# Other batch sizes, weights converted in wide pieces by a leaky ramp, the last chain on four quadrants, and a new order

## The chip, the cores and the metric

The kernel runs on one core of one Trainium2 chip. The metric is device time in microseconds of one execution, and the figure of a kernel is the median of its runs. The core has a matrix engine (PE, in the profile also TensorE), three engines for element work (DVE or VectorE, ACT or ScalarE, POOL or GpSimd), a queue that issues transfers (SP), and 16 DMA engines. SBUF is the memory that all engines work in; PSUM, eight banks of 512 columns, receives what PE computes.

## The reference

Two attention steps over 4 batches of 12480 tokens with 128 channels, and then a two-layer network on all 49920 tokens:

```python
def mab(q, kv):                      # softmax attention
    s = scale * (q @ kv.transpose(0, 2, 1))
    a = softmax(s)
    return a @ kv
h = mab(I, x)                        # I: 32 inducing rows; h: 32 x 128 per batch
x2 = mab(x, h)                       # 12480 x 128 per batch
y = x2 @ w_in                        # 128 -> 2048
g = 0 if y <= -1; y if y >= 1; (y + 1)**2 / 4 between
out = g @ w_out                      # 2048 -> 128
```

x is float32; w_in and w_out arrive as float64, which no engine computes in.

## The kernel before, in words

Below, "batch" is one of the 4 batches b of the reference, and "chunk" one of the 25 token batches of 512 or 480 into which each b is cut (SIZES); GROUPS joins up to four chunks whose attention is computed side by side in the four quadrants of 32 partitions.

**Weights (load_f32, load_in, load_out).** Each 256-column piece of a float64 weight is fetched as pairs of 32-bit words and turned into float32 by a row of steps: ACT scales the high word (L908), DVE or POOL clamps (L914), DVE shifts (L919), takes the sign bit over from the raw word (L923), masks (L929) and multiplies with the low word (L934), and DVE or POOL joins the two parts (L945 for w_in, L942 for w_out). Then w_out is kept as an fp32 copy w_f (L975) or as an upper and a lower fp32r half, w_hi (L984) and w_lo (L982).

**Summary of a batch (summarize).** Per group: x is loaded (L1008; for b = 0 it is transposed by PE, L1018, and copied by ACT, L1023; for the others it is loaded a second time in 32-column pieces, L1036, and transposed by DVE, L1039), scored against the inducing rows (L1061), its maximum taken (L1066), exponentiated with the group's own maximum (L1078), transposed (L1103, L1113), multiplied with x (L1122) and kept in hs (L1129). After all seven groups a chain of small steps c1 to c12 (L1163 to L1208) finds the maximum over groups, the factor of each group, the sum, and adds the groups up in PE with one matmul for each (L1204). The result is hT (32 summary rows). It is multiplied with w_in (L1230), so that the first layer of the network acts on 32 rows instead of on 128 channels; hw holds the product as fp32r halves, spread by DMA (L1251).

**Attention of a group (attend; attend_first for chunk 0).** Scores, softmax over 32 columns on DVE, ACT and POOL (L1279 to L1322); the weights aT go into chunk rows by DMA (L1346).

**Chunk (chunk).** For each of eight k: two hidden matmuls (L1465), a rectifier on ACT (rise, L1473), a square on ACT (L1459), max and min against the hidden value on DVE (bound, L1478). For k in SPLIT (six of eight; in the very last chunk END, five of eight) the result is split: the upper half hi is written by DVE (L1504), ACT (L1502) or POOL (L1498), the lower half lo by POOL alone (L1509), and PE projects with three fp32r matmuls for each 128 rows (L1540); the other k are projected in fp32 with w_f. A transpose (L1552) and four stores (L1556) end a chunk. Until the first projection PE is kept busy by 128-column matmuls of the identity that nobody reads (L1568).

**What sets the order.** All operations are put down in program order by add(), which names engine, slots and needs. ORDER gives each a rank on its own engine (even numbers; an odd one allows a pair of neighbouring PSUM banks to be handled by one instruction), and ON chooses the engine where there is a choice. Plan.order then emits one queue per engine in that order; every engine works through its queue strictly in order. SLOTS says how many buffers each pool has; FIRST says which pools the 25 first x tiles use. In the first chunk, the lower half on POOL also waits for all eight pieces of w_out (the list ahead).

## Time and profile before

| | us |
|---|---|
| median of 3 runs | 1698.43 (1698.05 to 1699.51) |
| span of the profiled execution | 1695.9 |
| PE busy | 1680.8 (99%) |
| ACT busy | 1643.5 (97%) |
| DVE busy | 1629.2 (96%) |
| POOL busy | 1615.0 (95%) |
| DMA, mean over the span | 62 GB/s, 105.65 MB |

Busy time is the union of instruction durations of an engine; neighbours can overlap, and a matmul's end is modelled. A timeline row gives start and length in us from the start of the span, the line, what is written and read, and in brackets the idle time before it with what ended it. A group row gives the count, then busy time and mean length in ns, then idle time before and its releasers.

### The profile page before, as it was taken

How to read it: one execution, taken by the hardware profiler on the slowest of the kernel's cores; microseconds unless marked ns; L12 is line 12 of the kernel's file. 1: busy time of each engine (PE TensorE's matmuls, PEld its weight loads, DVE VectorE, ACT ScalarE, POOL GpSimd, SP SyncE). 2: the span in 40 equal slices, each digit the busy share in tenths (PEclk: the TensorE clock that was granted, in tenths of full speed). 3: DMA queues.
4: the chain of work that ended last, by engine and by line, in shares of the span. 5: the costliest groups of instructions: out<-in, count | busy, mean ns of one | idle time of the engine just before them, and what ended most of it. 6: DMA issues, size and time to landing. Idle time of an engine off the chain costs nothing.

```text
span 1695.9 us, 24904 instructions
## 1 busy us (share of the span) xinstructions
PE 1680.8 (99%) x7770; PEld 1193.0 (70%) x7770; DVE 1629.2 (96%) x2057; ACT 1643.5 (97%) x2232; POOL 1615.0 (95%) x859
## 2 busy tenths in 40 slices
PE   8999999999999999999999999999999999999998
PEld 6766767677766766677776676677777666667776
DVE  6999999999999999999999999999999999999997
...
GB/s 233 127 53 69 96 66 58 67 60 70 79 67 57 67 64 73 52 68 63 69 87 53 77 52 47 92 54 55 39 33 63 35 24 38 35 28 35 37 28 25
DMA packets 427094, 105.65 MB, mean 62 GB/s; under 512 B 369842, under 2 KB 412434, under 8 KB 426962
## 3 DMA queue, kind: packets, MB, share of 16 engines
...
q8 instruction: 61, 1.00, 0.3%
q14 instruction: 71, 0.58, 0.1%
q10 hardware_dynamic: 1232, 0.40, 0.1%
...
## 4 chain that ended last, share of the span: by engine, by line
PE 79%; DVE 7%; ACT 7%; issue 3%; POOL 2%; SPq 1%; DMA 1%; DVEq 0%; ACTq 0%; POOLq 0%
PE banks L1540 55%; PE banks L1465 17%; DVE w L1478 4%; ACT w L1473 3%; ACT w L1459 3%; DVE hi L1504 2%; PE banks L1122 2%; POOL lo L1509 1%; PE banks L1568 1%; PE banks L1061 1%; PE banks L1279 1%; DVE oT L1552 1%; PE banks L1103 1%; SPq L1036 1%; PE banks L1018 1%
## 5 line engine op out<-in xcount | busy, mean ns | idle before, releaser
L1509 POOL TENSOR_TENSOR lo<-w,hi 128x1024 fp32r<-128x1024 f32 (+1 forms) x599 | 1392.4, 2353 | 17.7 <-PE banks L1540 4.2
L1478 DVE SCALAR_TENSOR_TENSOR w<-banks,w 128x512 f32<-128x512 f32 (+3 forms) x1105 | 953.2, 899 | 19.1 <-ACT w L1459 13.6
L1473 ACT ACTIVATE w<-banks 128x512 f32<-128x512 f32 (+3 forms) x1160 | 814.8, 755 | 12.2 <-PE banks L1465 8.3
L1459 ACT ACTIVATE w<-w 128x1024 f32<-128x1024 f32 (+1 forms) x800 | 820.2, 1054 | 6.4
L1465 PE MATMUL banks<-aT,hw 128*128 128x512 f32 (+1 forms) x1600 | 592.2, 430 | 0.6 <-DVE w L1478 0.4
L1540 PE MATMUL banks<-hi,w_lo 128*128 128x512 f32 (+1 forms) x1198 | 497.4, 415 | 4.0 <-DVE oT L1552 2.9
L1504 DVE TENSOR_REDUCE hi<-w 128x1024 fp32r<-128x1024 f32 (+1 forms) x406 | 475.5, 1179 | 9.0 <-PE banks L1540 0.9
L1540 PE MATMUL banks<-hi,w_hi 128*128 128x512 f32 (+1 forms) x1198 | 462.9, 386 | 0.0
L1540 PE MATMUL banks<-lo,w_hi 128*128 128x512 f32 (+1 forms) x1198 | 460.3, 431 | 1.0 <-DVE oT L1552 0.8
L1465 PEld LDWEIGHTS banks<-aT,hw 128*128 128x128 f32 x1600 | 295.8, 188 | 154.8 <-DVE w L1478 48.5
L1540 PE MATMUL banks<-w,w_f 128*128 128x512 f32 (+1 forms) x804 | 397.5, 581 | 0.0
L1540 PEld LDWEIGHTS banks<-lo,w_hi 128*128 128x128 f32 x1198 | 223.4, 188 | 103.5 <-issue 49.8
L1540 PEld LDWEIGHTS banks<-hi,w_lo 128*128 128x128 f32 x1198 | 225.0, 188 | 89.4 <-issue 27.1
L1540 PEld LDWEIGHTS banks<-hi,w_hi 128*128 128x128 f32 x1198 | 225.1, 188 | 54.6 <-issue 16.0
L1540 PEld LDWEIGHTS banks<-w,w_f 128*128 128x128 f32 x804 | 150.8, 188 | 45.0 <-issue 18.8
L1498 POOL TENSOR_SCALAR hi<-w 128x1024 fp32r<-128x1024 f32 (+1 forms) x141 | 145.4, 1033 | 4.5 <-DVE w L1478 1.4
L1552 DVE STREAM_TRANSPOSE oT<-banks 128x512 f32<-128x512 f32 (+1 forms) x100 | 69.8, 698 | 8.6 <-PE banks L1540 7.5
L1502 ACT CAST hi<-w 128x1024 fp32r<-128x1024 f32 (+1 forms) x52 | 53.6, 1034 | 0.5 <-DVE w L1478 0.5
L1039 DVE STREAM_TRANSPOSE xT<-xr 128x512 f32<-128x512 f32 (+1 forms) x75 | 51.0, 684 | 1.4 <-issue 0.9
L1322 POOL TENSOR_TENSOR a<-a,ahi 128x512 fp32r<-128x512 f32 (+3 forms) x28 | 35.5, 1269 | 1.0 <-ACT ahi L1319 1.0
L1061 PE MATMUL banks<-xT,indT 128*32 128x512 f32 (+1 forms) x200 | 30.5, 592 | 0.0
L1311 POOL TENSOR_TENSOR s<-s,sm 128x512 f32<-128x512 f32 (+3 forms) x28 | 29.0, 1034 | 1.1 <-DVE sm L1308 1.0
(127 smaller groups left out, 545.7 us busy)
## 6 DMA issues: line engine op xcount, KB each, us to landing
out<-oT SPq DMA_DIRECT2D x240, 64.0 KB, 2.2
...
xr<-in_x SPq DMA_DIRECT2D x120, 60.0 KB, 2.4
```

Of the source, the lines that this page charges most:

```text
L1039: nc.vector.transpose(make(xT[b, c])[:, : CW[c]], xr.tile[:, : NB[c]].rearrange("c n i -> c (n i)"))
L1061: nc.tensor.matmul(p[q * M : (q + 1) * M, :cw], indT, xT[b, c].tile[:, :cw], start=True, stop=True)
L1459: nc.scalar.activation(w.tile[:, :, :cw], w.tile[:, :, :cw], AF.Square, scale=0.5)
L1465: nc.tensor.matmul(make(h)[:, :cw], hw[b][ft // 4].tile[:, ft % 4 * P : (ft % 4 + 1) * P], aT[b, c].tile[:, :cw], start=True, stop=True,)
L1473: each(of, i, hs_, lambda h, to: nc.scalar.activation(to, h, AF.Relu, bias=1.0), cw, w)
L1478: lambda h, t: nc.vector.scalar_tensor_tensor(t, h, 1.0, t, op0=ALU.max, op1=ALU.min), cw, w,
L1498: nc.gpsimd.tensor_scalar(make(hi)[:, :, :cw], w.tile[:, :, :cw], 1.0, 0.0, op0=ALU.mult, op1=ALU.add)
L1502: nc.scalar.copy(make(hi)[:, :, :cw], w.tile[:, :, :cw])
L1504: nc.vector.tensor_reduce(make(hi)[:, :, :cw], w.tile[:, :, :cw].unsqueeze(3), axis=AX.X, op=ALU.max)
L1509: nc.gpsimd.tensor_sub(make(lo)[:, :, :cw], w.tile[:, :, :cw], hi.tile[:, :, :cw].bitcast(F32))
L1540: nc.tensor.matmul(acc.tile[:, :cw], wt[k][:, i, :], g.tile[:, i, :cw], start=first, stop=(acc.parts == 0),)
L1552: nc.vector.transpose(make(oT)[:, :nb].rearrange("c n i -> c (n i)"), acc.tile[:, :cw])
```

## The change

SIZES becomes 20 chunks of 512 and 5 of 448 tokens, and the seventh group holds one chunk. For b = 0 every x tile has four token blocks; 448-token chunks order their columns the other way round (n i instead of i n). The first 16 x tiles lie two by two in the hi and lo slots, the other nine in xn, so that the eight w slots take the raw weights. Weights are converted in eight pieces of 512 columns. The scaling step is a leaky ramp (Prelu) with a slope of 2^32 for negative values, so that the shift by three keeps the sign and the step that took it over from the raw word is gone; w_f, w_hi and w_lo are written for two k at once, on ACT or POOL. The copies of x for b = 0 may be on DVE. In the summary, the maximum over the first six groups is taken before the last group is scored; the last group is scored in all four quadrants, so that each has its maximum; the first six groups are added up on DVE (merge, six steps), and two matmuls are left where there were seven. Chunks 0 and 1 use END (five of eight k split), the list ahead is gone, and the square has its factor moved into the rectifier. ORDER and ON are new. In the new ON the uppers of the chunks are 391 on DVE, 66 on ACT and 140 on POOL; the squares stay on ACT; of the 25 copies of x, 13 are on DVE.

Read from the new ORDER, SP issues x0 to x19 of b = 0 (11 and 12 swapped), w_in 0, x20 to x24, w_in 1, 3, 2, w_out 0, 3, 1, 2; POOL makes ident first; DVE's queue from the clamp of w_in 0 to the copy of hT has 39 steps, and ACT's rebias steps stand in five groups between exponentials.

The diff, cut to its core; of ORDER and ON nothing is shown:

```diff
-FIRST = ["w", "hi", "lo"] * 2 + ["xn"] * 9 + ["w", "hi", "w", "lo", "w", "w", "hi", "w", "lo", "w"]
-SIZES = [512] * 15 + [480] * 10
-GROUPS = [[0, 1, 2, 3], [4, 5, 6, 7], [8, 9, 10, 11], [12, 13, 14], [15, 16, 17, 18], [19, 20, 21, 22], [23, 24]]
+FIRST = ["hi"] * 4 + ["lo"] * 4
+SIZES = [512] * 20 + [448] * 5
+GROUPS = [[0, 1, 2, 3], [4, 5, 6, 7], [8, 9, 10, 11], [12, 13, 14, 15], [16, 17, 18, 19], [20, 21, 22, 23], [24]]
...
-    WS = 2 * P
...
+    WS = 4 * P
+
+    def load_f32(src, pools, dst=None):
+
...
-            else:
-                mag[0] = make(home, [P, WS], F32)
-            nc.scalar.activation(mag[0], high, AF.Copy, scale=2.0**-112)
+            nc.scalar.activation(make(home, [P, WS], F32), high, AF.Prelu, scale=2.0**-112, alpha=2.0**32)
...
             most = 122879.9921875 * 2.0**-112
             on = nc.vector if single.engine == "DVE" else nc.gpsimd
-            on.tensor_scalar(mag[0], mag[0], most, -most, op0=ALU.min, op1=ALU.max)
...
         def shift():
...
-            if other is not home:
-                top[0] = make(other, [P, WS], U32)
-            nc.vector.tensor_scalar(top[0], mag[0].bitcast(U32), 3, None, op0=ALU.logical_shift_left)
-
...
-        def upper():
-
-            nc.vector.scalar_tensor_tensor(
-                top[0], raw.tile[:, :, 1], 0x80000000, top[0], op0=ALU.bitwise_and, op1=ALU.bitwise_or
+            nc.vector.tensor_scalar(
+                make(other, [P, WS], U32), home.tile.bitcast(U32), 3, None, op0=ALU.logical_shift_left
...
         def weight():
 
-            nc.vector.tensor_scalar(
-                mag[0].bitcast(U32), top[0], 0xFF800000, None, op0=ALU.bitwise_and
-            )
+            nc.vector.tensor_scalar(home.tile.bitcast(U32), other.tile, 0xFF800000, None, op0=ALU.bitwise_and)
 
         def lower():
             nc.vector.scalar_tensor_tensor(
-                mag[0], raw.tile[:, :, 0], 2.0**-52, mag[0], op0=ALU.mult, op1=ALU.mult
+                home.tile, raw.tile[:, :, 0], 2.0**-52, home.tile, op0=ALU.mult, op1=ALU.mult
             )
 
...
-        f = add("SP", 740, 3500, fetch, [after], [raw], span=(700, math.inf))
-        v = add("ACT", 290, 430, rebias, [f], [home, raw])
-        v = single = add(dict(DVE=(268, 400), POOL=(420, 550)), 0, 0, to_single, [v], [home], alone=True)
-        v = add("DVE", 270, 400, shift, [v], [home, other], alone=True)
-        v = add("DVE", 418, 550, upper, [v], [raw, other], alone=True)
-        v = add("DVE", 263, 395, weight, [v], [home, other], alone=True)
-        v = add("DVE", 420, 550, lower, [v], [raw, home], alone=True)
-        both = 345 if dst is None else 470
-        joined = add(dict(DVE=(both, both + 130), POOL=(700, 850)), 0, 0, join, [v], [home, other], alone=True)
-        return joined, home, mag
-
-    w_hi, w_lo, w_f, w_made, whole_made = {}, {}, {}, {}, []
+                by = lambda a: a.rearrange("p (a b) -> p b a", b=4)
+                add_to(dst, by(home.tile), by(t))
+
+        f = add("SP", 1400, 4200, fetch, [], [raw], span=(700, math.inf))
+        v = add("ACT", 700, 840, rebias, [f], [home, raw])
+        v = single = add(dict(DVE=(400, 530), POOL=(770, 900)), 0, 0, to_single, [v], [home], alone=True)
+        v = add("DVE", 410, 540, shift, [v], [home, other], alone=True)
+        v = add("DVE", 400, 530, weight, [v], [home, other], alone=True)
+        v = add("DVE", 690, 820, lower, [v], [raw, home], alone=True)
+        both = 620 if dst is None else 800
+        joined = add(dict(DVE=(both, both + 130), POOL=(1300, 1450)), 0, 0, join, [v], [home, other], alone=True)
+        return joined, home
+
+    w_hi, w_lo, w_f, w_made, whole_made = {}, {}, {}, {k: [] for k in range(NP)}, []
     in_made = []
...
+    def load_out(j):
+        src = w_out[j * WS : (j + 1) * WS].rearrange("(p t) d -> p t d", t=4)
+        made, home = load_f32(src, ("xr", "oT"))
         whole_made.append(made)
...
+            _, m = copy("w_f", ks, F32, w_f)
+            for k in ks:
+                w_made[k].append(m)
+        ks = [k for k in pair if any(k in s for s in [SPLIT, END])]
+        if ks:
+            hi, m = copy("w_hi", ks, F32R, w_hi)
+            lo = held_for("w_lo", ks, F32R, w_lo)
+
+            def lower(ks=ks):
+                nc.gpsimd.tensor_sub(lo, value(ks), hi.bitcast(F32))
+
+            wait = 650 if len(ks) == 1 else 1300
+            m = add("POOL", wait, wait + 100, lower, [m], [home])
+            for k in ks:
+                w_made[k].append(m)
...
-                pool = FIRST[c % len(FIRST)] if b == 0 else "xn"
...
+                if b == 0 and c < 2 * len(FIRST):
+                    xn[c] = xn[c - 1] if c % 2 else Slot(FIRST[c // 2])
+                else:
+                    xn[c] = in_turn("xn")
+
+                def fetch(c=c):
+                    if b == 0 and c < 2 * len(FIRST):
+                        if c // 2 not in whole:
+                            whole[c // 2] = make(xn[c], [P, 2, T, C], F32)
+                        rows[c] = whole[c // 2][: CW[c] // T, c % 2]
+                    else:
+                        rows[c] = make(xn[c], [CW[c] // T, T, C], F32)
+                    nc.sync.dma_start(rows[c], rows_of(b, c))
+
+                got[c] = [add("SP", 900 if b else 700, 3200 if b else 3500, fetch, [], [xn[c]], span=later)]
...
-                    xT_made[b, c] = add("ACT", cost(c, 46, 0.95), cost(c, 186, 0.95), put, [m], [xT[b, c], pt])
+                    by = []
+                    ways = dict(
+                        ACT=(cost(c, 46, 0.95), cost(c, 186, 0.95)), DVE=(cost(c, 66, 1.05), cost(c, 206, 1.05))
+                    )
+                    xT_made[b, c] = add(ways, 0, 0, lambda put=put, by=by: put(by=by), [m], [xT[b, c], pt])
+                    by.append(xT_made[b, c])
...
+            tail = g == NG - 1
...
+                for q, c in enumerate(cs * Q if tail else cs):
...
+                if tail:
+                    nc.vector.tensor_reduce(ml, p1.tile[:, :cw], axis=AX.X, op=ALU.max)
+                    nc.vector.tensor_scalar(nb, ml, mb, -SCALE, op0=ALU.max, op1=ALU.mult)
+                    return
...
+        def c7():
+            nc.vector.tensor_mul(fs, fe, sg[:, : NG - 1])
+            nc.vector.tensor_reduce(early, fs, axis=AX.X, op=ALU.add)
+
+        def merge(g):
+            if g == 0:
+                nc.vector.tensor_scalar(he, hs[:, 0, :], fe[:, :1], None, op0=ALU.mult)
+                return
+            nc.vector.scalar_tensor_tensor(he, hs[:, g, :], fe[:, g : g + 1], he, op0=ALU.mult, op1=ALU.add)
+
+        def c8():
+            nc.scalar.activation(fall, mb, AF.Exp, bias=state["nb", b], scale=SCALE)
+
+        def c9():
+            nc.vector.scalar_tensor_tensor(tot, early, fall, sg[:, NG - 1 :], op0=ALU.mult, op1=ALU.add)
+
+        def c10():
+            nc.tensor.matmul(make(s_t)[:, :1], fold_f, tot, start=True, stop=True)
+
+        def c11():
+            nc.vector.tensor_scalar(rs, s_t.tile[:, :1], 1e-9, None, op0=ALU.add)
+            nc.vector.reciprocal(rs, rs)
+            nc.vector.tensor_scalar(ff[:, 0, :], fold[:, 0, :], fall, rs, op0=ALU.mult, op1=ALU.mult)
+            nc.vector.tensor_scalar(ff[:, 1, :], fold[:, 0, :], rs, None, op0=ALU.mult)
+
+        def c12(n):
+            p = s_h.tile or make(s_h)
+            nc.tensor.matmul(p[:, :M], (he, hs[:, NG - 1, :])[n], ff[:, n, :], start=(n == 0), stop=(n == 1))
+
...
+            if g == NG - 1:
+                o = add("DVE", 80, 230, c1, [*mosts, folded])
+                o = add("PE", 60, 300, c2, [o], [s_m])
+                o = add("DVE", 200, 340, c3, [o], [s_m])
+                o = add("PE", 130, 310, c4, [o], [s_b], tiled=True)
+                o = bound = add("DVE", 160, 310, c5, [o], [s_b])
+                factors = add("ACT", 100, 250, c6, [o])
             s = score(g)
             if last:
                 gather(g - 1, last)
             last = s
+        e = add("DVE", 220, 350, c7, [factors, *summed[:-1]])
+        for g in range(NG - 1):
+            o = add("DVE", 190, 320, lambda g=g: merge(g), [o if g else state.get("chain"), factors, lasts[g]], alone=g > 0)
+        merged = o
         gather(NG - 1, last)
-
...
-        def c11(groups):
-            p = s_h.tile or make(s_h)
-            for g in groups:
-                nc.tensor.matmul(p[:, :M], hs[:, g, :], ff[:, g, :], start=(g == 0), stop=(g == NG - 1))
...
-        o = add("DVE", 300, 450, c7, [o, *summed], [s_f])
-        o = add("PE", 120, 300, c8, [o], [s_t])
-        o = add("DVE", 250, 400, c9, [o], [s_t])
-        o = add("DVE", 320, 450, c10, [o, state.get("ff")], [s_f])
-        o = add("PE", 1350, 1550, lambda: c11(range(NG - 1)), [o, *lasts[:-1]], [s_h])
-        state["chain"] = state["ff"] = o = add("PE", 225, 425, lambda: c11([NG - 1]), [o, lasts[-1]], [s_h])
-        hT_made[b] = add("DVE", 100, 240, c12, [o], [s_h])
+        o = fell = add("ACT", 100, 250, c8, [mosts[-1], bound])
+        o = add("DVE", 90, 220, c9, [o, e, summed[-1]])
+        o = add("PE", 120, 300, c10, [o], [s_t])
+        o = add("DVE", 420, 560, c11, [o, fell, state.get("chain")], [s_t])
+        o = add("PE", 225, 425, lambda: c12(0), [o, merged], [s_h])
+        state["chain"] = o = add("PE", 225, 425, lambda: c12(1), [o, lasts[-1]], [s_h])
+        hT_made[b] = add("DVE", 100, 240, c13, [o], [s_h])
...
-            split = k in (END if (b, c) == (B - 1, NCH - 1) else SPLIT)
+            split = k in (END if (b, c) == (B - 1, NCH - 1) or b == 0 and c < 2 else SPLIT)
+
+            by = []
+
+            def square(w=w, by=by):
+                v = w.tile[:, :, :cw]
+                if by[0].engine == "POOL":
+                    nc.gpsimd.tensor_mul(v, v, v)
+                else:
+                    nc.scalar.activation(v, v, AF.Square)
...
-                    each(of, i, hs_, lambda h, to: nc.scalar.activation(to, h, AF.Relu, bias=1.0), cw, w)
+                    each(of, i, hs_, lambda h, to: nc.scalar.activation(to, h, AF.Relu, bias=0.5, scale=0.5), cw, w)
...
-                ahead = [*whole_made, *(m for v in w_made.values() for m in v)] if (b, c) == (0, 0) else []
-                if ahead:
-                    del ways["POOL"]
-                l = add("POOL", cost(c, 0, 4.66), cost(c, 104, 4.66), lower, [u, *ahead], [lo, w, hi])
+                l = add("POOL", cost(c, 0, 4.66), cost(c, 104, 4.66), lower, [u], [lo, w, hi])
```

## Rows read from the trace of the kernel before

**Rows 1.** Stretches of the whole kernel: start:end, length, then busy us by engine.
```profile
core 0: us, PE busy (x) PEld busy (x) DVE busy (x) ACT busy (x) POOL busy (x), PEclk, DMA share, GB/s
...
5.00:17.00 12.00, 11.15 (x114) 8.77 (x113) 5.99 (x17) 8.70 (x20) 1.10 (x2) 1.00 1.02 375
...
17.00:30.00 13.00, 12.43 (x177) 9.17 (x175) 10.28 (x30) 10.52 (x28) 1.53 (x3) 1.00 1.02 285
...
45.00:66.90 21.90, 21.90 (x177) 19.22 (x176) 20.37 (x46) 17.88 (x30) 10.22 (x17) 1.00 0.55 136
...
66.90:1640.00 1573.10, 1567.54 (x6901) 1105.39 (x6900) 1534.74 (x1870) 1551.93 (x2072) 1547.57 (x799) 1.00 0.28 58
...
1640.00:1680.00 40.00, 40.00 (x165) 30.16 (x165) 39.86 (x46) 39.81 (x56) 39.83 (x21) 1.00 0.13 25
...
1680.00:1696.00 16.00, 10.87 (x40) 7.16 (x39) 6.45 (x8) 4.79 (x6) 8.23 (x4) 0.99 0.21 35
```

**Rows 2.** POOL's lower halves: group (busy, mean ns, idle), then timeline (start, length).
```profile
L1509 POOL TENSOR_TENSOR lo<-w,hi 128x1024 fp32r<-128x1024 f32 x360 | 857.1, 2411 | 9.2 <-DVE hi L1504 2.4 <-PE banks L1540 1.7 <-ACT w L1459 0.4
...
66.88 9.49 POOL L1509 TENSOR_TENSOR lo<-w,hi 128x1024 fp32r<-128x1024 f32 x4
...
1672.63 15.64 POOL L1509 TENSOR_TENSOR lo<-w,hi 128x960 fp32r<-128x960 f32 x7
```

**Rows 3.** Timeline of ACT in the steady part, two neighbours.
```profile
71.34 1.04 ACT L1502 CAST hi<-w 128x1024 fp32r<-128x1024 f32 x1
...
72.28 1.06 ACT L1459 ACTIVATE w<-w 128x1024 f32<-128x1024 f32 x1
```

**Rows 4.** Wait for x in the opening: timeline, then chain (start, length).
```profile
31.62 0.60 PE L1018 MATMUL banks<-ident,w 96*128 96x96 f32 x5 [0.88 <-DMA w<-in_x]
...
23.01 8.47 DMA w<-in_x
```

**Rows 5.** Groups of DVE's weight conversion, 5 to 60 us.
```profile
L923 DVE SCALAR_TENSOR_TENSOR oT<-hw,oT 128x256 uint32<-128x256 uint32 x3 | 1.2, 416 | 0.0
...
L929 DVE TENSOR_SCALAR oT<-oT 128x256 uint32<-128x256 uint32 x6 | 1.7, 288 | 0.1
...
L934 DVE SCALAR_TENSOR_TENSOR oT<-hw,oT 128x256 f32<-128x256 uint32 x3 | 1.2, 411 | 0.0
...
L945 DVE TENSOR_TENSOR w_in_sb<-aT,s 128x256 f32<-128x256 f32 x5 | 3.1, 615 | 0.0
```

**Rows 6.** Timeline, landmarks of the opening on PE and DVE.
```profile
40.77 1.75 PE L1204 MATMUL banks<-ff,hs 128*128 128x32 f32 x14
...
50.73 1.20 PE L1465 MATMUL banks<-aT,hw 128*128 128x512 f32 x4
...
42.55 0.19 DVE L1208 COPY hT<-banks 128x32 f32<-128x32 f32 x1 [0.61 <-PE banks L1204]
...
67.03 0.48 PE L1540 MATMUL banks<-hi,w_lo 128*128 128x512 f32 x1
```

**Rows 7.** Timeline of DVE and POOL, two pairs that overlap.
```profile
41.19 0.56 DVE L934 SCALAR_TENSOR_TENSOR oT<-xr,oT 128x256 f32<-128x256 uint32 x1
...
41.07 0.40 POOL L914 TENSOR_SCALAR oT<-oT 128x256 f32<-128x256 f32 x1 [0.56 <-ACT oT L908]
...
47.19 0.54 DVE L923 SCALAR_TENSOR_TENSOR oT<-xr,oT 128x256 uint32<-128x256 uint32 x1
...
47.05 0.40 POOL L914 TENSOR_SCALAR oT<-oT 128x256 f32<-128x256 f32 x1 [0.22 <-ACT oT L908]
```

**Rows 8.** Groups of the upper halves on DVE and ACT.
```profile
L1504 DVE TENSOR_REDUCE hi<-w 128x1024 fp32r<-128x1024 f32 x239 | 286.5, 1206 | 5.2 <-PE banks L1540 0.4
...
L1502 ACT CAST hi<-w 128x1024 fp32r<-128x1024 f32 x36 | 37.7, 1051 | 0.0
```

**Rows 9.** Group of ACT's table loads.
```profile
L1023 ACT ACT_TABLE_LOAD x1 | 1.3, 1283 | 1.2 <-PEq L1605 1.2
```

**Rows 10.** Group of the unsplit projections on PE.
```profile
L1540 PE MATMUL banks<-w,w_f 128*128 128x512 f32 x480 | 242.0, 592 | 0.0
```

256 lines of the change are left out of this document (127 added, 129 removed), and 988 rows, old and new, of the table ORDER.

## The prediction

> **What bounds the kernel now.** I read the table of stretches first [rows 1]. Its stretch 66.9 to 1640 us is the steady part: POOL is busy 98.4% of it (1547.57 of 1573.1), ACT 98.7%, DVE 97.6%, PE 99.6%, with the TensorE clock granted at 1.00, that is 2.4 GHz, all through. Such shares count durations, and durations overlap: an ACT instruction of 1.04 us is followed by the next one after 0.94 us [rows 3], so ACT's real need lies several per cent under its share, and PE's and DVE's durations overlap in the same way. POOL's do not: its last seven lower halves take 15.64 us, 2.23 each for 960 columns, which scaled to 1024 is 2.38, the group's mean of 2.41 [rows 2]. So POOL is the engine with the least slack, from its first lower half at 66.88 us [rows 2] to its last. The time is then the moment at which that stream begins, plus POOL's work, plus a tail of some 8 us.
>
> Before that moment stands the opening. The DMA engines are full to 30 us, at 375 GB/s while 512-token batches come and at 285 GB/s while the 96-partition batches of 480 come [rows 1]; the last x transfers are still waited for at 31.62 us, one of them 8.47 us under way [rows 4]. DVE is busy 5.99 of 12 us and then 10.28 of 13 us meanwhile [rows 1]: it waits for data. The first batch's summary h ends at 42.55 + 0.19 us, its first hidden matmul runs at 50.73, and the first projection only at 67.03 [rows 6]; PE's full column in 45 to 66.9 [rows 1] is mostly the idle matmuls of L1568. In 45 to 66.9 DVE is the busy one (20.37 of 21.9), half of it with weight conversion.
>
> **The change, part by part.** *x first, all weights with a slot of their own.* The new order has SP issue x0 to x19, w_in0, x20 to x24 and then the other seven weight pieces; 25 x and 8 pieces have 25 + 8 places, so no transfer waits for a slot. 20 x of 0.26 MB and one piece of 0.52 MB are 5.8 MB, 15.4 us at 375 GB/s [rows 1]; from about 2 us that is 17.5, with the ramp on ACT about 18.5 us. The 448-token batches use 112 partitions of 2 KB; which of the two rates they get no row shows, so the last x lands between 21 and 23 us, 8 to 10 us earlier than now.
>
> *DVE up to h.* From there DVE's new queue has 39 steps to the copy of h. Conversion: 14 one-input steps on 512 columns, which cost 0.29 at 256 [rows 5]; bounds 0.29 (all fixed) and 0.58 (all per column), I take 0.40, 5.6 us. Four products at 0.41 [rows 5], bounds 0.41 and 0.82, taken 0.65: 2.6. Two joins at 0.62 [rows 5], taken 0.9: 1.8. The rest (three maxima, three copies of x, the chain, six merges) I estimate at 8 us from steps of 0.2 to 0.7 us like those of [rows 5]. That makes 18 us, from 18.5 to 36.5, and 2.5 us for the chain's round trips: h at 39, 3.7 us earlier than 42.74. With all at the low bounds and no waits it is 34, with all at the high ones 42.7. ACT gives 13 of its 25 copies of x to DVE and has room. The shorter chain itself (two matmuls of a pair of factors after the last batch instead of 14 passes in 1.75 us [rows 6], the maximum of six groups taken early) is inside these 39 steps; where it saves PE a microsecond, DVE ends later anyway.
>
> *From h to POOL's first lower half.* Today 24.1 us (42.74 to 66.88). DVE has 27 conversion steps there: eleven at 0.29, sixteen at about 0.41 [rows 5], 9.8 us. In the new queue ten or eleven wide ones remain: five of 0.40, five of 0.65, a join of 0.9: 6.2. The masking step of 0.42 [rows 5] is gone, since the ramp keeps the sign. That is 3.6 us less, and the first lower half no longer waits for all eight pieces of w_out; but POOL has its own joins and copies in front of it, some 6 us from the last product on, so I count no more than DVE's 3.6. Together the stream begins 7 us earlier, at 60; bounds 12 and 0.
>
> *POOL's work.* Batches 0 and 1 take k = 7 unsplit: two lower halves of 2.41 us [rows 2] less, and by the choice letters one upper half less (140 on POOL for 141): -5.0 us with about 0.7 added for a weight copy behind the first lower half, bounds -5.9 and -4. PE pays for it with two unsplit pairs of 1.0 us a matmul [rows 10] in place of twelve short ones, under 4 us, in a queue that has room as long as POOL is last.
>
> *Batches of 512 and 448.* 12480 tokens and 25 batches as before, hence the same instructions and columns in the steady part; the seven groups' widths sum to 3520 for 3488, 1% of a minor part: nothing on POOL beyond 1 us.
>
> *Upper halves.* 406 on DVE become 391, 52 on ACT become 66. At 1.21 and 1.05 us [rows 8] DVE loses 18 us and ACT gains 15. Their cover is the slack just found; if it were gone ACT's 15 us would show.
>
> *The merges.* In each of batches 1 to 3 some ten small DVE steps that read SBUF alone are new beside POOL's stream (six merges, the sums, the two factors); today's chain there reads one operand from PSUM. The trace shows what such a step meets: a product that starts at 41.19 while POOL works from 41.07 to 41.47 lasts 0.56 in place of 0.41, and at 47.19 a masking step 0.54 in place of 0.42 while POOL works from 47.05 to 47.45 [rows 5, 7]: both end one normal step after POOL's instruction. Beside a lower half of 2.41 us a step would wait 1.2 us on average, 30 steps 36 us of DVE's time, bounds 0 and 72. POOL in turn waits for the small step, bounds 0 and 0.3 us each, I take 0.15: +4.5 us on POOL. The Trainium skill (SBUF — State Buffer, Who interferes with whom) says that VectorE and GpSimd share a pair of ports and that the one that has it keeps the other waiting for its whole instruction; the two rows agree, though only with POOL instructions of 0.4 us.
>
> **Sum.** 1695.9 - 7 - 5 + 4.5 = 1688.4 us of span. The median of the runs, 1698.43, lies 2.5 us over the span of the profiled execution; with that, 1691 us.
>
> **The rivals.** *The merges cost POOL nothing and the order packs as well:* 1698.4 - 7 - 5 = 1686. For it: DVE has lost 18 us of upper halves. Down to 1682 with an opening at its lower bound.
> *The opening stays as long as it is:* another step, such as PE's turning of x or the wide conversions at twice the narrow price, holds h at 42; then only 2 of the 7 us remain: 1698.4 - 2 - 5 + 4.5 = 1696, no change that can be told. For it: DVE's queue in front of h gains 13 copies of x and the merges.
> *The merges stall DVE (slower):* 36 us of waiting in an in-order queue on which every hidden bank depends. If a share s of it reaches the end, the time is 1698.4 - 12 + 36 s: the gain is gone at s = 0.33, and at s = 0.5 it is 1704. Against it: the waits come in three places, each with DVE slack of a few us around it; for it: DVE has 2.4% idle by its share, 38 us in all, and must find 36 there.
> *The ramp needs another table:* the trace has one table load, 1.28 us [rows 9], for all functions used so far. If the ramp is not in that table, each change between it and the exponentials loads again; by the new ACT queue five groups of ramps stand between exponentials, ten loads, 13 us in front of and around h, of which about half finds ACT idle: the opening's 7 us are gone, and some more, 1700 to 1704. The Trainium skill gives such a switch 2.66 us with its drain (ScalarE: Activation LUTs, What ACT_TABLE_LOAD costs); by that it would be 27 us on ACT and an end near 1710, and no run here shows which functions share a table.
> *ACT is the bound:* if ACT's 98.7% were real, its 15 us would come on top of a start 4 us earlier: 1709. Against it stand the starts 0.94 us apart [rows 3].
>
> **How the numbers follow.** Forecast (1691): 0.46. Merges free: 0.18. Opening unchanged: 0.13. Merges stall DVE: 0.14, of which a third lands near no change. Table loads: 0.05. ACT, or an order that packs worse: 0.04. I call 0.2%, 3.4 us, what a measurement can tell, so faster means under 1695.0 and slower over 1701.8. Forecast and free merges give 0.64 faster; the unchanged opening and the mild stalls 0.18 the same; the rest 0.18 slower. For 8 in 10 the range reaches from 1682, the opening at its lower bound, to 1703, short of a stall share of a half.
>
> **What would show it.** Right: the last x waited for by about 23 us, h near 39, POOL's first lower half near 60, 597 of them, one table load in the trace, DVE merges that last longer than 0.3 us by up to 2.4. The sum is wrong if POOL's share after its start falls under 98%: then the order or the merges took the gain. It is also wrong if POOL starts at 60 and the end does not move: then POOL is not the bound. A start at 66 with h near 39 would say that POOL's own weight work, or the projections' wait for it, decides the opening.

## The result, and the profile after

The changed kernel is slower: 1714.34 us (1713.46 to 1715.32) against 1698.68 us (1698.05 to 1699.51) for the kernel before, measured side by side; the ratio is 1.0092, 95% interval 1.008 to 1.0103. The profiled execution spans 1711.7 us, where that of before spanned 1695.9.

First the landmarks of the prediction. Each row is the answer for one source line: engine, operation, names, count, shortest/median/longest duration in ns, first and last start in us.

```profile
L1254 DVE COPY hT<-banks x1: 180/180/180, 39.0 to 39.0; 128x32 f32<-128x32 f32 x1
...
L1578 POOL TENSOR_TENSOR lo<-w,hi x597: 2058/2406/2477, 61.5 to 1703.1; 128x1024 fp32r<-128x1024 f32 x160, 128x896 fp32r<-128x896 f32 x39
```

The copy of h stands at 39.0 (before at 42.55, [rows 6]), GpSimd's first lower half at 61.5 (before 66.88, [rows 2]), and there are 597 lower halves. Up to there the opening did what it was meant to do. The table of stretches tells where the time went then (start:end, length, busy us of each engine with its instructions, granted TensorE clock, DMA share, GB/s):

```profile
core 0: us, PE busy (x) PEld busy (x) DVE busy (x) ACT busy (x) POOL busy (x), PEclk, DMA share, GB/s
...
66.90:1640.00 1573.10, 1552.89 (x6794) 1085.94 (x6793) 1526.52 (x1847) 1543.78 (x2052) 1522.23 (x784) 1.00 0.28 57
...
285.00:485.00 200.00, 195.31 (x879) 139.61 (x878) 190.49 (x246) 192.36 (x266) 189.33 (x103) 0.99 0.30 61
485.00:685.00 200.00, 198.74 (x883) 136.94 (x882) 192.70 (x230) 198.21 (x262) 196.61 (x99) 1.00 0.30 61
685.00:885.00 200.00, 196.25 (x912) 138.78 (x910) 194.66 (x249) 195.00 (x271) 190.24 (x104) 1.00 0.31 64
885.00:1085.00 200.00, 198.86 (x877) 139.01 (x878) 194.57 (x231) 198.11 (x257) 197.06 (x100) 1.00 0.33 67
1085.00:1285.00 200.00, 194.07 (x902) 135.66 (x901) 194.54 (x239) 190.65 (x268) 188.10 (x99) 1.00 0.24 47
```

The same three stretches with a batch end in them, of the kernel before:

```profile
285.00:485.00 200.00, 200.00 (x923) 144.87 (x922) 192.41 (x251) 197.12 (x276) 196.61 (x105) 1.00 0.33 70
...
685.00:885.00 200.00, 199.86 (x938) 143.99 (x938) 193.89 (x244) 195.75 (x268) 195.70 (x105) 1.00 0.32 67
...
1085.00:1285.00 200.00, 199.06 (x937) 144.16 (x936) 192.68 (x236) 193.85 (x260) 195.03 (x104) 1.00 0.23 47
```

Between the batch ends GpSimd (POOL) is about as full as before (98.3 and 98.5% in the two stretches, for 98.5 and 98.6). In each stretch with a batch end it now stands idle for 9.8 to 11.9 us of 200, where it was 3.4 to 5.0 before. TensorE loses beside it, and VectorE (DVE) looks about as busy as before. Over the whole steady part POOL's share is 1522.23 / 1573.1 = 96.8%, for 98.4% [rows 1]. That was the sign set down for "the order or the merges took the gain".

A second way to see it: take the start of each chunk's output transpose and compare it with the kernel before at the same token. At the 22nd chunk of batch 0 the changed kernel is 3.5 us ahead (428.5 for 432.0); at the first chunk of batch 1 it is 5.5 behind, at that of batch 2 9.1, at that of batch 3 15.9, and in the middle of the batches the distance stays within about 2 us of one level. So 3.5 + 15.9 = 19.4 us are lost where a batch ends and the chain of the next one runs.

What happens there is seen best at the end of batch 0. The rows are the timeline: start, length, engine, line, operation; in brackets the idle time before and what ended it.

```profile
429.66 0.97 DVE L1245 TENSOR_SCALAR ff<-fold,fall,rs 128x32 f32<-128x32 f32 x1
430.55 3.19 DVE L1246 TENSOR_SCALAR ff<-fold,rs 128x32 f32<-128x32 f32 x1
433.65 0.61 DVE L1543 SCALAR_TENSOR_TENSOR w<-banks,w 128x448 f32<-128x448 f32 x1
```
```profile
424.30 6.29 POOL L1578 TENSOR_TENSOR lo<-w,hi 128x896 fp32r<-128x896 f32 x3
430.55 1.12 POOL L1381 TENSOR_TENSOR a<-a,ahi 32x448 fp32r<-32x448 f32 x1
431.64 2.06 POOL L1578 TENSOR_TENSOR lo<-w,hi 128x896 fp32r<-128x896 f32 x1
436.96 2.12 POOL L1578 TENSOR_TENSOR lo<-w,hi 128x896 fp32r<-128x896 f32 x1 [3.26 <-ACT hi L1571]
```
```profile
434.32 0.97 PE L1530 MATMUL banks<-aT,hw 128*128 128x448 f32 x2 [2.94 <-DVE w L1543]
```
```profile
435.02 0.98 ACT L1538 ACTIVATE w<-banks 128x448 f32<-128x448 f32 x2 [3.91 <-PE banks L1530]
```

A fold (L1246, a step of 128x32) that lasts 0.23 us when nothing holds it up lasts 3.19 us here, and ends when POOL's second instruction ends at 433.70. Behind it on DVE's queue stands the bound of a hidden block; TensorE waits 2.94 us for the bank that this bound frees, ScalarE 3.91 us for the hidden matmul, POOL 3.26 us for the next upper half. One small step has emptied all four engines. All such steps of batches 1 to 3, as groups (count, busy us, mean ns, idle time before):

```profile
L1231 DVE SCALAR_TENSOR_TENSOR he<-hs,fe,he 128x128 f32<-128x128 f32 x15 | 12.0, 798 | 0.1
L1237 DVE SCALAR_TENSOR_TENSOR tot<-early,fall,sg 128x1 f32<-128x1 f32 x3 | 3.8, 1256 | 0.0
L1246 DVE TENSOR_SCALAR ff<-fold,rs 128x32 f32<-128x32 f32 x3 | 3.6, 1216 | 0.0
L1229 DVE TENSOR_SCALAR he<-hs,fe 128x128 f32<-128x128 f32 x3 | 2.5, 845 | 0.0
L1224 DVE TENSOR_TENSOR fs<-fe,sg 128x6 f32<-128x6 f32 x3 | 2.5, 823 | 0.0
L1245 DVE TENSOR_SCALAR ff<-fold,fall,rs 128x32 f32<-128x32 f32 x3 | 2.1, 716 | 0.1
```

30 steps take 26.5 us. Their shortest durations, when POOL leaves them alone, are 0.33 us (a merge), 0.29 (the first of them), 0.14 (the product of factors and sums), 0.21 (the sum) and 0.23 (a fold; 0.30 with two factors), some 8.2 us in all. So about 18.3 us are waits. The merges in the form shortest/median/longest, in ns:

```profile
L1231 DVE SCALAR_TENSOR_TENSOR he<-hs,fe,he x15: 322/352/2634, 376.1 to 1272.3; 128x128 f32<-128x128 f32 x15
```

A wait is counted as busy time, which is why DVE's column above shows nothing.

### The profile page after: what moved, and what is told of

Its sections match the earlier page's. It is cut to its first block, busy times and chain, and to the rows that moved or that the text cites. A ratio compares the mean times of both kernels' runs of the same rounds, so it can differ in the third digit from the quotient of the medians.

```text
span 1711.7 us, 24841 instructions
## 1 busy us (share of the span) xinstructions
PE 1683.9 (98%) x7713; PEld 1188.8 (69%) x7713; DVE 1640.0 (96%) x2040; ACT 1648.2 (96%) x2220; POOL 1610.4 (94%) x849
## 4 chain that ended last, share of the span: by engine, by line
PE 86%; DVE 7%; ACT 2%; issue 2%; DMA 1%; SPq 1%; POOL 0%; DVEq 0%; ACTq 0%; POOLq 0%
PE banks L1606 61%; PE banks L1530 19%; DVE w L1543 3%; PE banks L1167 1%; PE banks L1338 1%; PE banks L1098 1%; DVE hi L1573 1%; ACT w L1524 1%; ACT w L1538 1%; DVE oT L1618 1%; PE banks L1634 1%; PE banks L1044 1%; PE banks L1148 1%; DMA xr<-in_x 1%; DVE he L1231 0%
## 5 line engine op out<-in xcount | busy, mean ns | idle before, releaser
L1543 DVE SCALAR_TENSOR_TENSOR w<-banks,w 128x1024 f32<-128x1024 f32 (+3 forms) x1098 | 950.8, 902 | 22.4 <-ACT w L1524 15.7
L1530 PE MATMUL banks<-aT,hw 128*128 128x512 f32 (+1 forms) x1600 | 601.7, 432 | 12.4 <-DVE w L1543 10.0
L1606 PE MATMUL banks<-hi,w_lo 128*128 128x512 f32 (+1 forms) x1194 | 507.1, 425 | 4.1 <-DVE oT L1618 3.1
L1573 DVE TENSOR_REDUCE hi<-w 128x1024 fp32r<-128x1024 f32 (+1 forms) x391 | 459.5, 1180 | 11.5 <-PE banks L1606 2.9
L1606 PE MATMUL banks<-w,w_f 128*128 128x512 f32 (+1 forms) x812 | 404.0, 582 | 0.1
L1571 ACT CAST hi<-w 128x1024 fp32r<-128x1024 f32 (+1 forms) x66 | 67.7, 1026 | 0.5 <-DVE w L1543 0.4
L1370 POOL TENSOR_TENSOR s<-s,sm 128x512 f32<-128x512 f32 (+3 forms) x28 | 28.8, 1030 | 1.3 <-DVE sm L1367 0.8
```

What stands on the lines that cost most here:

```text
L1530: nc.tensor.matmul(make(h)[:, :cw], hw[b][ft // 4].tile[:, ft % 4 * P : (ft % 4 + 1) * P], aT[b, c].tile[:, :cw], start=True, stop=True,)
L1543: lambda h, t: nc.vector.scalar_tensor_tensor(t, h, 1.0, t, op0=ALU.max, op1=ALU.min), cw, w,
L1571: nc.scalar.copy(make(hi)[:, :, :cw], w.tile[:, :, :cw])
L1573: nc.vector.tensor_reduce(make(hi)[:, :, :cw], w.tile[:, :, :cw].unsqueeze(3), axis=AX.X, op=ALU.max)
L1606: nc.tensor.matmul(acc.tile[:, :cw], wt[k][:, i, :], g.tile[:, i, :cw], start=first, stop=(acc.parts == 0),)
```

## Experiments

Two theories were put against each other. **A:** the waits of these steps reach the end of the kernel. **B:** the new order packs worse at the batch ends, whoever does these steps. Ratios below are to the kernel before, with the 95% interval; its median beside the runs lay between 1698.3 and 1699.0 us, so a difference between two runs below that weren't measured together is good to about 1 us at best. The diffs are cut to their core.

### The steps away from VectorE, both kinds and each alone

```diff
 def c9():
+    if b:
+        nc.scalar.activation(tot, early, AF.Identity, bias=sg[:, NG - 1 :], scale=fall)
+        nc.scalar.activation(fg, fg, AF.Identity, scale=fall)
+        return
 def merge(g):
+    if b:
+        nc.scalar.activation(fg[:, g, :], fold[:, 0, :], AF.Identity, scale=fe[:, g : g + 1])
+        return
 def c11():           # behind the reciprocal
+    if b:
+        nc.scalar.activation(ff[:, 1, :], fold[:, 0, :], AF.Identity, scale=rs)
+        nc.scalar.activation(fg, fg, AF.Identity, scale=rs)
+        return
 def c12(n):
+    if b and n == 0:
+        for g in range(NG - 1):
+            nc.tensor.matmul(p[:, :M], hs[:, g, :], fg[:, g, :], start=(g == 0), stop=False)
+        return
```

> The changed kernel; in batches 1 to 3 the six merges go (ScalarE scales the fold by each group's early factor instead, six steps of 128x32, and TensorE takes the six groups one by one, as the kernel before did) and the steps on the sum and on the folds go from VectorE to ScalarE. So no wide VectorE step between two SBUF operands is left in these chains but the product of factors and sums; batch 0 and the order of the work stay. Theory A (VectorE waits for GpSimd in these steps, and what it waits reaches the end): the steps' time above their normal adds up to about 17 us in the trace, and all of it comes back but for some 3 us of added matmuls and ScalarE steps: 1696 to 1702. Theory B (the new order packs worse at the batch ends, whatever engine does these steps): 1711 to 1718, with the gaps of GpSimd still there.

Measured 1705.39 us, 1.0040 (1.0027 to 1.0053), between the two expectations. In this form and in the third one the folds of the early groups come out other than in the changed kernel, so the summary of batches 1 to 3 differs; kind, size and number of the instructions are as told.

The factors alone (the sum and the two folds to ScalarE, the merges left as they are):

```diff
 def c9():
+    if b:
+        nc.scalar.activation(tot, early, AF.Identity, bias=sg[:, NG - 1 :], scale=fall)
+        return
 def c11():           # behind the reciprocal
+    if b:
+        nc.scalar.activation(ff[:, 1, :], fold[:, 0, :], AF.Identity, scale=rs)
+        nc.scalar.activation(ff[:, 0, :], ff[:, 1, :], AF.Identity, scale=fall)
+        return
```

> The changed kernel; in batches 1 to 3 only the steps on the sum (one) and on the folds (two) go from VectorE to ScalarE; the merges stay. Theory A: these nine steps lasted about 7.5 us above their normal (0.2 us each), so 1705 to 1709. Theory A with a share that grows for the last steps, because the next batch's first matmuls stand behind them: down to 1702. Theory B: 1712 to 1716.

Measured 1705.98 us, 1.0043 (1.0027 to 1.0058). The nine steps had waited 7.5 us (3.8 + 3.6 + 2.1 less 2.0 of work), and 8.4 us came back: theory A, with a share of 1.1.

The merges alone (the folds of the six groups by ScalarE and six products on TensorE as in the first run, the rest on VectorE):

```diff
 def c11():           # behind the reciprocal
+    if b:
+        nc.vector.tensor_scalar(fg, fg, fall, rs, op0=ALU.mult, op1=ALU.mult)
```

> The changed kernel; in batches 1 to 3 only the six merges go (ScalarE scales the folds, TensorE takes the groups one by one); the steps on the sum and on the folds stay on VectorE. Theory A: the merges lasted about 9 us above their normal, and give that back but for some 3 us of added matmuls and ScalarE steps: 1706 to 1710. Theory B: 1713 to 1719, the added work on top.

Measured 1711.40 us, 1.0076 (1.0063 to 1.0090). The merges had waited 8.7 us and only 3 came back, and both kinds together gave hardly more than the factors alone. This was less than theory A said. Either the waits of the merges cost little, or what replaced them (18 ScalarE steps and 15 products) cost much; the runs further down speak for the second, without settling it.

### What such a wait costs, in the kernel before

Ten VectorE steps per batch that nobody needs, in batches 1 to 3, in a form with two SBUF operands, and as a control in a form with one:

```diff
+    def extra():   # with two SBUF operands
+        nc.vector.scalar_tensor_tensor(spare[:, :P], fold_f, 1.0, spare[:, :P], op0=ALU.mult, op1=ALU.max)
+    def extra():   # the control
+        nc.vector.tensor_reduce(spare[:, :P], fold_f.unsqueeze(2), axis=AX.X, op=ALU.max)
     def keep():
         nc.scalar.copy(hs[:rows, g, :], ph.tile[:rows, :C])
+        if b: extra()
     def c9():
         nc.vector.reciprocal(rs, rs)
+        if b: extra(), extra(), extra()
```

> The kernel before; with ten more VectorE steps per batch in batches 1 to 3 (multiply and maximum of two SBUF operands, 128x128, nobody needs the result), one where each group's sum is kept and three behind the reciprocal: about as many as the changed kernel has there, in the old order. Theory A: 30 steps, each waiting 0.6 us on average as in the changed kernel, reach the end nearly whole: 1712 to 1720. My own forecast's share of a third: 1704 to 1708. Theory B (such steps are not what costs): 1698 to 1703.

> The control of the run before it: the same 30 steps at the same places as a reduction with one SBUF operand (128x128, about 0.3 us each). Theory A: 9 us of VectorE work at 96% busy and no waits: 1699 to 1703. Theory B: the same as its partner with two operands, within 1 us.

Measured 1739.57 us, 1.0240 (1.0223 to 1.0256), and for the control 1701.34 us, 1.0015 (1.0006 to 1.0025). Then the same steps in the middle of the batches, two ahead of each output transpose of chunks 6 to 10, and their control:

```diff
 def turn():          # of chunk(b, c)
+    if b and c in (6, 7, 8, 9, 10): extra(), extra()
     nc.vector.transpose(make(oT)[:, :nb].rearrange("c n i -> c (n i)"), acc.tile[:, :cw])
```

> The kernel before; with the same 30 steps of two SBUF operands elsewhere: two ahead of the output transpose of chunks 6 to 10 of batches 1 to 3, away from the chain. Theory A with a share that doesn't depend on the place: the same time as with the steps at the chain, within 3 us. Theory A with a share that is high only at the batch ends: 1700 to 1706 here.

> The control of the 30 steps in the middle of the batches: the same places, as a reduction with one SBUF operand (0.27 us each). If the waits alone made the 58.6 us there: 1700 to 1703, as with the control at the chain. If a step ahead of the output transpose is dear for another reason: 1710 or more.

Measured 1757.01 us, 1.0340 (1.0325 to 1.0356), and 1706.02 us, 1.0043 (1.0030 to 1.0057). The groups of the added steps, at the chain and its control, then in the middle and its control:

```profile
L858 DVE SCALAR_TENSOR_TENSOR spare<-fold,spare 128x128 f32<-128x128 f32 x30 | 36.7, 1222 | 0.2
```
```profile
L858 DVE TENSOR_REDUCE spare<-fold 128x128 f32<-128x128 f32 x30 | 8.2, 274 | 0.2
```
```profile
L858 DVE SCALAR_TENSOR_TENSOR spare<-fold,spare 128x128 f32<-128x128 f32 x30 | 46.3, 1542 | 0.5
```
```profile
L858 DVE TENSOR_REDUCE spare<-fold 128x128 f32<-128x128 f32 x30 | 8.4, 279 | 0.5
```

At the chain 36.7 - 8.2 = 28.5 us of waits cost 1739.57 - 1701.34 = 38.2 us; in the middle 46.3 - 8.4 = 37.9 us cost 51.0. Both times one us waited costs about 1.35 us at the end, so the place makes no difference that can be told. The steps themselves, 8.2 and 8.4 us of work, cost 2.9 us at the chain and 7.2 in the middle. Four expectations missed: the waits were longer than 0.6 us each, they are no dearer at the batch ends, my forecast's share of a third is out by a factor of four, and the control in the middle is 3 us slower than its first range. Why a us of waiting costs more than a us was not tried; the granted clock goes with it: the two runs with waits have a mean of 0.989 and 0.988, their controls 1.000.

```profile
core 0: 1755.9 us, clock 0.988
```
```profile
core 0: 1704.9 us, clock 1.000
```

### The same steps in forms that don't wait

The control shows the way out: keep the steps on VectorE, but in other forms (free_steps). The product and the folds read one operand from PSUM, and the sum takes its factors as per-partition scalars on a single column. One wide SBUF operand in place of two isn't enough by itself: the two folds and the first merge (TENSOR_SCALAR) had only one, and lasted 0.72, 1.22 and 0.85 us on average where 0.30, 0.23 and 0.29 were enough.

```diff
 def c6():
     nc.scalar.activation(fe, mg[:, : NG - 1], AF.Exp, bias=nm, scale=SCALE)
+    if b: nc.scalar.activation(s_b.tile[:, 8 : 8 + NG - 1], mg[:, : NG - 1], AF.Exp, bias=nm, scale=SCALE)
 def c7():
-    nc.vector.tensor_mul(fs, fe, sg[:, : NG - 1])
+    nc.vector.tensor_mul(fs, s_b.tile[:, 8 : 8 + NG - 1] if b else fe, sg[:, : NG - 1])
 def c9():
+    if b: nc.vector.tensor_scalar(tot, early, fall, sg[:, NG - 1 :], op0=ALU.mult, op1=ALU.add); return
 def c11():           # behind the reciprocal, p = s_t.tile
+    if b:
+        nc.vector.tensor_copy(p[:, 1:2], rs)
+        by = p[:, 1:2].to_broadcast([P, M])
+        nc.vector.scalar_tensor_tensor(ff[:, 0, :], by, fall, fold[:, 0, :], op0=ALU.mult, op1=ALU.mult)
+        nc.vector.scalar_tensor_tensor(ff[:, 1, :], by, 1.0, fold[:, 0, :], op0=ALU.mult, op1=ALU.mult)
+        return
-e = add("DVE", 220, 350, c7, [factors, *summed[:-1]])
+e = add("DVE", 220, 350, c7, [factors, *summed[:-1]], [s_b] if b else [])
```

> The changed kernel; in batches 1 to 3 the chain's VectorE steps but the merges get a form in which at most one wide operand lies in SBUF, on VectorE still: the factors come a second time into PSUM and are multiplied from there, the sum takes its factors as per-partition scalars, the reciprocal is put into PSUM and the folds are made from it. What is known so far: a wait on such a step cost the kernel before 1.36 us at the end for each us waited (38 us over its control for 28 us). Theory A: in the changed kernel these steps waited about 9 us in all (7.5 without the product of factors and sums), so 1714.3 less 1.1 to 1.4 times that, 1701 to 1704.5; and less than 1706, since ScalarE no longer gets nine added steps. Theory B (half of the loss is the order's, not the waits'): 1705 to 1708.

Measured 1705.16 us, 1.0031 (1.0000 to 1.0061): at the edge of both expectations. The product lasts 0.14 us each time here and the folds 0.25 and 0.18; the merges still wait 8 us. Then (free_all) without the merges too: ScalarE scales the factors into the bank of the sum, one VectorE step makes six folds from there, TensorE takes six products, and ScalarE makes the fold of the last group.

```diff
 def c10():
     nc.tensor.matmul(make(s_t)[:, :1], fold_f, tot, start=True, stop=True)
+    if b: nc.scalar.activation(s_t.tile[:, 8 : 8 + NG - 1], fe, AF.Identity, scale=fall)
 def c11():
+        nc.vector.scalar_tensor_tensor(
+            fg, s_t.tile[:, 8 : 8 + NG - 1].unsqueeze(2).to_broadcast([P, NG - 1, M]), rs,
+            fold[:, :1, :].to_broadcast([P, NG - 1, M]), op0=ALU.mult, op1=ALU.mult)
```

> As free_steps, and the six merges go too: the factors of the six groups, scaled by ScalarE into PSUM, make six folds in one VectorE step, and TensorE takes the groups one by one, as in the kernel before (15 more small products in all, 3 us, and two more ScalarE steps for each batch). Theory A: all of about 17 us of waits go, at 1.36 us each 23 us, less some 3 to 5 us of added work: 1694 to 1697. Theory B (half of the loss is the order's): 1701 to 1706. If the added matmuls and not the waits are what kept the run without shared steps at 1705, it stays at 1704 to 1706.

Measured 1703.95 us, 1.0031 (1.0018 to 1.0043). No step waits any more (the nine that are left last 2.4 us, each within 0.02 us of its shortest duration), and yet 7 us more are left than theory A allowed. Theory B seemed to gain. But the last line of the diff of free_steps, which free_all keeps, has a side effect: it holds the bank of the maxima up to the product, a few us longer, and the banks that the hidden matmuls get are picked from what is free. So the held bank was tried alone, with everything else as in the changed kernel, and then free_all without it (with the product from SBUF, as in the changed kernel):

```diff
-e = add("DVE", 220, 350, c7, [factors, *summed[:-1]])
+e = add("DVE", 220, 350, c7, [factors, *summed[:-1]], [s_b] if b else [])
```

> The changed kernel with its waits, but the PSUM bank of the maxima is given back after the product of factors and sums and not after the step ahead of it, a few us later in batches 1 to 3; no instruction differs but for the banks they name and which rises and bounds are joined. If the held bank is what took the gain in free_all: 1719 to 1724. If the order's packing is the cause and banks don't matter: 1713 to 1716.

> As free_all, but the product of factors and sums is taken from SBUF again, as in the changed kernel, so that no PSUM bank is held for it. In the trace of free_all the bank that is held a few us longer had changed which banks the hidden matmuls get, and with that the joined rises (413 for the changed kernel's 438) and the joined bounds (471 for 502). Theory A (waits, and in free_all the held bank in their place): only the product's waits are left, 1 us each in three batches, so below free_all's 1704, at 1696 to 1700. Theory B (the order costs what is left): 1704 to 1709, free_all plus these waits.

Measured 1718.51 us, 1.0118 (1.0103 to 1.0134), for the held bank: 4.2 us more than the changed kernel. And 1701.52 us, 1.0013 (1.0004 to 1.0022), without it: 12.8 us less than the changed kernel, and between the two expectations. The bounds of the hidden blocks, wide (both banks at once) and narrow, first of the changed kernel, then with the bank held:

```profile
L1543 DVE SCALAR_TENSOR_TENSOR w<-banks,w 128x1024 f32<-128x1024 f32 x403 | 482.1, 1212 | 10.1 <-ACT w L1524 8.7 <-POOL lo L1578 0.2 <-issue 0.2
...
L1543 DVE SCALAR_TENSOR_TENSOR w<-banks,w 128x896 f32<-128x896 f32 x98 | 104.1, 1076 | 4.4 <-ACT w L1524 2.2 <-POOL lo L1578 0.8 <-issue 0.5
...
L1543 DVE SCALAR_TENSOR_TENSOR w<-banks,w 128x448 f32<-128x448 f32 x124 | 71.8, 609 | 0.8 <-ACT w L1524 0.6
```
```profile
L1543 DVE SCALAR_TENSOR_TENSOR w<-banks,w 128x1024 f32<-128x1024 f32 x395 | 472.7, 1213 | 10.8 <-ACT w L1524 9.5 <-issue 0.2 <-POOL hi L1567 0.2
...
L1543 DVE SCALAR_TENSOR_TENSOR w<-banks,w 128x448 f32<-128x448 f32 x170 | 97.5, 609 | 1.1 <-ACT w L1524 0.6
L1543 DVE SCALAR_TENSOR_TENSOR w<-banks,w 128x896 f32<-128x896 f32 x75 | 80.2, 1079 | 3.8 <-ACT w L1524 2.0 <-issue 0.5 <-POOL lo L1578 0.5
```

403 + 98 wide bounds have become 395 + 75: 31 pairs of banks are no longer neighbours and take two instructions, at 448 tokens 2 x 0.61 us for 1.08. Not all of the 4.2 us is shown to come from this: the thirty steps of the chain also last 28.8 us there in place of 26.5, the granted clock has a mean of 0.997 for 0.999, and these weren't separated. Cleaner is free_all, where no step waits and 31 pairs are gone as well: it is 2.4 us slower than the same without the held bank, though that one still waits 3.1 us. free_steps has lost the same 31 pairs; what they cost there wasn't measured. Without the held bank, the steps that were changed and the one that was not:

```profile
L1225 DVE TENSOR_TENSOR fs<-fe,sg 128x6 f32<-128x6 f32 x3 | 3.6, 1185 | 0.0
L1254 DVE SCALAR_TENSOR_TENSOR fg<-banks,rs,fold 128x192 f32<-128x192 f32 x3 | 1.3, 417 | 0.1
L1241 DVE TENSOR_SCALAR tot<-early,fall,sg 128x1 f32<-128x1 f32 x3 | 0.8, 269 | 0.0
```

Only the product from SBUF still waits, 3.1 us. To take that as well, it was made in six steps on single columns:

```diff
 def c7():
+    if b:
+        nc.vector.tensor_scalar(early, fe[:, :1], sg[:, :1], None, op0=ALU.mult)
+        for g in range(1, NG - 1):
+            nc.vector.tensor_scalar(early, fe[:, g : g + 1], sg[:, g : g + 1], early, op0=ALU.mult, op1=ALU.add)
+        return
```

> As the run without a held bank, and the product of factors and sums is made by six VectorE steps on single columns with per-partition scalars, a form that didn't wait in the last runs; some 0.8 us more VectorE work in each chain. Theory A: no wait is left in the chains of batches 1 to 3, 1693 to 1698, which is level with the kernel before or better. Theory B: 1704 to 1708.

Measured 1702.27 us, 1.0022 (1.0013 to 1.0030): nothing gained, a miss. Five more VectorE steps in a row per chain cost as much as the waits they replace: the product and its sum took 4.0 us of VectorE's time with the waits, the six steps take 4.65 without.

### What is left over

The merges' place taken by the first group alone:

```diff
-        for g in range(NG - 1):
+        for g in range(1):
             nc.tensor.matmul(p[:, :M], hs[:, g, :], fg[:, g, :], start=(g == 0), stop=False)
```

> As the run without a held bank, but TensorE takes the first group alone in batches 1 to 3; the products of the five other groups are left out, so this part of the first softmax's sums is missing, and the 15 products of 128x128 by 128x32 with their weight loads are gone that replaced the merges. What the changed kernel would take if its merges neither waited nor cost anything. If these products are what is left of the gap (some 1.2 us in each chain, on the path to the next batch's h): 1697 to 1699. If something else of the order holds the batch ends: 1700.5 to 1702.

Measured 1699.49 us, 1.0005 (0.9996 to 1.0014): the 15 added products are worth 2.0 us, 1.4 by the ratios, whose intervals overlap. With them put aside, the waits that are gone (18.3 - 3.1 = 15.2 us) gave back 12.8 + 2.0 = 14.8 us, a share of about 1.0. For the merges alone the runs don't agree so well. From free_steps to free_all their 8.0 us of waits go, and 1.2 us come back, 3.2 with the products, a share of 0.4. And the first run, with 24 more ScalarE steps and six fewer on VectorE than the run without a held bank and the same waits left, is 3.9 us slower than it. So for the factors the share is shown, for the merges only that it lies between 0.4 and 1.

The last run left out the stores of the last four chunks of batches 0 to 2 and of the first three of batches 1 to 3, to empty SP's queue at the batch starts.

```diff
 def store(k, queue):
+    if b < B - 1 and c >= 21 or b and c < 3:
+        return
```

> As the run without a held bank; the stores of the last four chunks of batches 0 to 2 and of the first three chunks of batches 1 to 3 are left out (that part of the result isn't written), 84 of SP's DMA issues at some 0.6 us each. SP issues nearly without a pause from 450 to 490 us in the trace of the changed kernel, and VectorE waits there for the pieces of x, 3.6 us in all in the run without a held bank. If these waits reach the end as the others did: 1697 to 1699. If they are hidden behind something: 1700.5 to 1702.

Measured 1698.67 us, 1.0000 (0.9991 to 1.0008): 2.9 us less than with all stores. What VectorE waited for, 75 to 1640 us, with all stores and with fewer (us in all, times, longest):

```profile
DVE xT L1075 <- DMA xr<-in_x: 3.6, 4, 1.4
```
```profile
DVE xT L1075 <- DMA xr<-in_x: 1.7, 2, 1.1
```

By the ratios it is 2.2 us, with intervals that just overlap, by the spans of the two profiled executions 2.0. The two waits at the starts of batches 1 and 2 are gone, the two at 80 and 90 us, where no store was left out, remain. In the kernel before this wait was 0.5 us in all, in the changed kernel 4.1. The x pieces of the next batch, the halves of hw and the stores meet on SP's queue; in the changed kernel SP issues one DMA after the other, some 0.6 us each, from 450 to 490 us (60 in 40 us, 51 in the kernel before). So this wait, too, seems to reach the end; but fewer stores also free the queue for the halves of hw and the weights aT, and these weren't tried apart. It is the order's, and a small part of theory B is right. The comparison by output transposes says the same: the run without a held bank goes from 3.2 us ahead at the 22nd chunk to 2.1, 3.5 and 4.1 us behind at the first chunks of batches 1 to 3, so 7 us are still lost at the batch ends, where it was 19.

No version was found that beats the kernel before. With all its steps but the product in forms that don't wait, the change comes out 0.13% behind it.

## Why the prediction was wrong

**The opening was right in its steps.** h at 39 was forecast and came at 39.0; the lower halves were to begin at 60 (bounds 55 to 67) and began at 61.5. The last wait for x ends at 6.2 us and the last turning of x starts at 25.0, where 23 was forecast for the last wait. The wide conversions cost 0.42 and 0.68 us and the joins 1.08, taken at 0.40, 0.65 and 0.9. With steps a little dearer than taken and x earlier than taken, that h agrees to 0.1 us is luck in part. One table load is in the trace, so the table rival fell:

```profile
L1056 ACT ACT_TABLE_LOAD x1 | 1.3, 1283 | 1.2 <-PEq L1671 1.2
```

**What the opening is worth was mis-sized.** The sum counted 7 us for the earlier start of the lower halves and 5 for fewer of them. The start is 5.4 us earlier, but the first projection runs at 66.22, where it was 67.03 ([rows 6]), and the first output transpose at 81.3, where it was 83.2. At the 22nd chunk the kernel is 3.5 us ahead, not 12. The first projection and the first two output transposes of the changed kernel, and the same two transposes before:

```profile
66.22 0.39 PE L1606 MATMUL banks<-hi,w_lo 128*128 128x512 f32 x1
```
```profile
L1618 DVE STREAM_TRANSPOSE oT<-banks x2: 705/711/717, 81.3 to 97.9; 128x512 f32<-128x512 f32 x2
```
```profile
L1552 DVE STREAM_TRANSPOSE oT<-banks x2: 708/712/717, 83.2 to 100.2; 128x512 f32<-128x512 f32 x2
```

So the sum's premise, that the time follows from the moment at which POOL's stream begins, failed within the first chunk: of 5.4 us there are 1.9 left at its end. What held the first projection wasn't tried. On POOL itself the trace shows where time went: up to 368 us it does 30 upper halves where it did 26, 4.2 us at 1.05, though over the whole run it is 140 for 141, and between 66.9 and 100 it stands idle for 2.6 us, where it was 0.1 before. Whether either cost anything at the end wasn't tried.

**The step that failed is the merges,** with the other small steps of the chain: the wait they bring to VectorE's queue was put at nothing. The forecast charged them to POOL, 0.15 us each, 4.5 in all. It expected merges that last up to 2.4 us longer, but left the price of this on VectorE's queue to a rival. In the timeline above POOL doesn't wait: 424.30 to 430.55 holds three lower halves back to back, and the next two instructions follow without a gap; and the longest of all 597 lower halves is 2.48 us, with a median of 2.41. The wait falls on VectorE. The rival "the merges stall DVE" is what happened, with 14 of 100, and both of its sizes were out. Thirty steps was right. The wait of a step came out at 18.3 / 30 = 0.61 us and not 1.2, since many of them meet no lower half or only its end. And the share of it that reaches the end was taken as a third to a half, because of VectorE's slack of a few us around each place: it is 1.1 for the factors and about 1.0 for all the waits that went in the changed kernel, with the merges alone less sure (0.4 to 1), and 1.35 in the kernel before. By the rival's own formula with these sizes and the forecast's gain of 12 the time would be 1698.4 - 12 + 18.3 = 1704.7; the measured 1714.3, 11 us beyond the upper end of the range, needs a gain of 2.4 in place of the 12. Two rows were read too freely as well, without a part in the miss. The product and the masking step end 0.28 us after POOL's instruction [rows 7], not one normal step of 0.41 after it, and an unsplit projection is 0.59 us a matmul [rows 10], not 1.0.

**Why there was no slack.** The prediction read "2.4% idle, 38 us" as room that a wait could fill. The idle time of an engine whose queue is in order and whose bounds free TensorE's banks wasn't room here: at 430.55 the bound stood behind the fold, and within 0.9 us ScalarE and TensorE stood too. Where TensorE stood for 2.94 us the granted clock fell as well (below).

**What was left out altogether** is the late x pieces: the prediction checked the x transfers of the opening, not those of the next batch, whose issues the new order lays beside the halves of hw and the stores on SP. They cost 2.0 to 2.9 us.

**The other rivals.** ScalarE as the bound: not so, it is idle for 5 to 9 us of each stretch with a batch end. The order packs worse: true for the x pieces. With neither waits nor added products nor late pieces the sum of the runs is 1714.3 - 14.8 - 2.9 - 3.1 (the product's waits, at a share of 1.0) = 1693.5; the three parts were measured in different kernels and weren't run together, so this is an estimate. The forecast without its 4.5 us for the merges says 1686.4; the 7 us between them are about what the opening's 12 us fell short by. That the estimate lies near the forecast's 1691 is luck.

The Trainium skill (SBUF — State Buffer, Who interferes with whom) says that a VectorE instruction with two SBUF inputs, or one in a mode that takes both port pairs, contends with GpSimd, and one with at most one SBUF input outside these modes doesn't. The rows here agree: two-input merges 0.80 us on average, the one-input reduction 0.27, the product 0.82 from SBUF and 0.14 with one factor in PSUM. The folds and the first merge have one wide SBUF input and waited too; this fits if they ran in such a mode, which no row shows. The page adds that whoever issues first has the pair for its whole instruction. Here a VectorE step that stood at 430.55 was passed over again at 431.64, when POOL's next instruction began; in this the measurement goes further than the page.
